# One load of x moves from SyncE's queue to GpSimd's, behind two accumulating transfers

## The chip, the cores and the metric

The kernel runs on one core of one Trainium2 chip. A core has five engines that run side by side: TensorE (PE in the profile; its weight loads are PEld), VectorE (DVE), ScalarE (ACT), GpSimd (POOL) and SyncE (SP). Sixteen DMA engines move data between the chip's large memory and the core's on-chip memory. A transfer is issued by one of the engines; those of SP and of GpSimd go through different queues, and both are served by the same sixteen DMA engines. The metric is the device time of one execution in microseconds (us), as a median over runs. Lower is better.

## What is computed

The input x has 8 batches of 4224 rows of 192 numbers. A causal convolution over the rows with 7 taps comes first: the 192 columns are 8 heads of 24, and each head has one set of softmaxed tap weights. Its result y is then normalized over the 192 columns, multiplied by a 192 x 768 matrix, cut at zero, multiplied by a 768 x 192 matrix, and added to y.

```python
w = np.exp(weight - weight.max(-1, keepdims=True)); w /= w.sum(-1, keepdims=True) + 1e-09
x_unf = x_pad[:, idx, :].reshape(B, S, K, H, group)       # 7 shifted copies of x
y = np.einsum('hk,bskhg->bshg', w, x_unf).reshape(B, S, D)
xn = (y - mu) / np.sqrt(var + 1e-06) * g_ln
out = y + np.maximum(xn @ w_ch1, 0.0) @ w_ch2
```

All of it is in 32-bit floats.

## The kernel before

**Groups.** The 4224 rows of a batch are spread over the 128 partitions, 33 consecutive rows to each. A group is a stretch of these 33 rows (n rows on every partition). Batch 0 is cut into groups 0 to 3 with n = 6, 7, 8 and 12; each later batch into two with n = 16 and 17. That makes 18 groups. Group 4 (16 rows) and group 5 (17 rows) are batch 1.

**Steps of a group.** `load_x` brings the rows of x and the six rows ahead of them into a tile `xg`, of which there are two buffers: x of group 5 takes the buffer of x of group 3. `first_tap` (L336, ScalarE) multiplies x by tap 0 into the tile `y`, also with two buffers, so that y of group 5 takes the buffer of y of group 3. `second_tap` multiplies by tap 1 into a separate tile `tb` (L349, ScalarE) and adds that to y by two accumulating transfers issued by GpSimd (L352), one for each half of the rows. `conv` adds the other taps on VectorE (L363), one instruction for each tap and head, `transpose` (L374, VectorE) turns y for the matmuls, and `store_y` (L431) writes y to the output. `up` makes the 768 hidden values on TensorE (L473), and ScalarE cuts them at zero into the tile `ht` (L485), in six blocks. The down step multiplies back (L509 or L553), and the scaled result is added to the output by accumulating transfers of GpSimd (`add_to_out`, L630).

**Two down steps.** Groups 0 to 2 use a plain one (`down`). From group 3 on `down_fast` does with seven smaller products (L553, 72 matmuls each) what would take eight. For these it needs sums and differences of quarters of `ht`, which VectorE makes (`half_sum`, L531, three instructions each). One is made ahead of the products; three are made behind the fourth product, in place, over quarters that the earlier products have read. The fifth product reads the first of these. Between the products ScalarE copies each result out (L558), and a few of the first and second taps of the group two ahead stand between these copies in its program (`some_taps`).

**Order.** It is written out by hand, and each engine works through its own program in that order. In the main loop, iteration g loads x of group g + 2, does `up(g)` on TensorE, meanwhile the taps of group g + 1 on VectorE, and then the down step of group g. Iteration 2 is the last with the plain down step: there both taps of group 4 are made whole on ScalarE (`first_tap(4)`, `second_tap(4)`), and y of group 3 is stored by GpSimd's queue, behind the two accumulating transfers. In iteration 3 VectorE does taps 2 to 4 of group 4 (24 instructions), the first half sum, taps 5 and 6 (16 instructions), the transpose, and then the three half sums of group 3's down step. The first tap of group 5 comes in that down step, on ScalarE behind the copies of the first product.

**Queues.** SP's program has the loads of x and nearly all stores of y. GpSimd's has the accumulating transfers of the second taps and of the output, and the one store of y of group 3. A transfer that has to wait (for a buffer, for data) holds up all that stands behind it in the program of the engine that issues it.

Of the kernel before, what the change touches and what calls it, by code (L numbers as in the profile page):

```python
# [16 lines left out]
def kernel(  # L17
# [27 lines left out]
    nc = tc.nc  # L45
# [27 lines left out]
    NG = len(groups)  # L73
# [25 lines left out]

    xg = {}  # L100

    def load_x(g):
        b, j0, n = groups[g]
        t = xpool.tile([P, J + PAD, D], F32, tag="xg", name=f"xg{g}")
        xg[g] = t
        flat = t.rearrange("p j d -> p (j d)")
        if j0:
            nc.sync.dma_start(
                out=flat[:, 0 : (n + PAD) * D], in_=xr[b, :, (j0 - PAD) * D : (j0 + n) * D]
            )  # L110
            return
        if b:

            nc.sync.dma_start(
                out=flat[:, 0 : (PAD + n) * D],
                in_=bass.AP(
                    tensor=x.tensor, offset=(b * S - PAD) * D, ap=[[R * D, P], [1, (PAD + n) * D]]
                ),
            )
            nc.gpsimd.memset(t[0:1, 0:PAD, :], 0.0)  # L120
            return
        nc.gpsimd.memset(t[0:1, 0:PAD, :], 0.0)
        nc.sync.dma_start(out=flat[:, PAD * D : (PAD + n) * D], in_=xr[b, :, 0 : n * D])
        for p0, p1 in ((16, P), (1, 16)):
            nc.sync.dma_start(  # L125
                out=flat[p0:p1, 0 : PAD * D],
                in_=xr[b, p0 - 1 : p1 - 1, (R - PAD) * D : R * D],
            )
# [196 lines left out]
    def first_tap(g, on_act=True, heads=(0, H)):  # L325
        n = groups[g][2]
        if g == 1:

            y[g] = y[0][:, groups[0][2] :]
        elif heads[0] == 0:  # L330
            y[g] = ypool.tile([P, J, D], F32, tag="y", name=f"y{g}")
        for h in range(*heads):
            cs = slice(h * GRP, h * GRP + GRP)
            dst, src, tap = y[g][:, 0:n, cs], xg[g][:, 0:n, cs], taps[:, h, 0:1]
            if on_act:
                nc.scalar.mul(dst, src, tap)  # L336
            else:
                nc.vector.tensor_scalar(out=dst, in0=src, scalar1=tap, scalar2=None, op0=ALU.mult)
# [3 lines left out]
    def second_tap(g, heads=(0, H)):  # L342

        n = groups[g][2]
        if heads[0] == 0:
            tb[g] = bpool.tile([P, J, D], F32, tag="tb", name=f"tb{g}")
        for h in range(*heads):
            cs = slice(h * GRP, h * GRP + GRP)
            nc.scalar.mul(tb[g][:, 0:n, cs], xg[g][:, 1 : 1 + n, cs], taps[:, h, 1:2])  # L349
        if heads[1] == H:  # L350
            for j1, j2 in ((0, n // 2), (n // 2, n)):
                nc.gpsimd.dma_start(  # L352
                    out=y[g][:, j1:j2].rearrange("p j d -> p (j d)"),
                    in_=tb[g][:, j1:j2].rearrange("p j d -> p (j d)"), accum_op=ALU.add,
                )

    def conv(g, k0=1, k1=K, heads=H):
        n = groups[g][2]
        t = xg[g]
        for k in range(k0, k1):  # L360
            for h in range(heads):
                cs = slice(h * GRP, h * GRP + GRP)
                nc.vector.scalar_tensor_tensor(  # L363
                    out=y[g][:, 0:n, cs], in0=t[:, k : k + n, cs], scalar=taps[:, h, k : k + 1],
                    in1=y[g][:, 0:n, cs], op0=ALU.mult, op1=ALU.add,
                )

    def transpose(g):
        n = groups[g][2]
        if g == 1:  # L370
            yt[g] = yt[g - 1][:, groups[0][2] :]
        else:
            yt[g] = tpool.tile([P, J, NC, C], F32, tag="yt", name=f"yt{g}")
        nc.vector.transpose(  # L374
            yt[g][:, 0:n].rearrange("p j c t -> p (j c t)"),
            y[g][:, 0:n].rearrange("p j d -> p (j d)"),
        )
# [3 lines left out]
    def moments(g):  # L381

        n = groups[g][2]
        if g % 2:
            sums[g] = sums[g - 1][:, groups[g - 1][2] :]
        else:
            sums[g] = spool.tile([P, 2 * J, nc.vector.BN_STATS_DIM], F32, tag="st", name=f"st{g}")
        for j in range(n):
            nc.vector.bn_stats(out=sums[g][:, j, :], in_=y[g][:, j, :])  # L389
# [39 lines left out]
    def store_y(g, queue=nc.sync):  # L429
        b, j0, n = groups[g]  # L430
        queue.dma_start(  # L431
            out=outr[b, :, j0 * D : (j0 + n) * D], in_=y[g][:, 0:n].rearrange("p j d -> p (j d)")
        )
# [61 lines left out]
    def down(g):  # L495


        n = groups[g][2]
        t = ht[g][1]
        po[g] = []  # L500
        order = [(c, js) for c in range(NC) for js in blocks(g)]
        if g + 1 == NG:
            order = [(c, slice(fast[g], n)) for c in range(NC)]
        for c, js in order:
            w = (js.stop - js.start) * C
            bank = psum.tile([P, 512], F32, tag="ps", name=f"po{g}_{c}_{js.start}")
            for f in range(NF):
                for q in range(NQ):
                    nc.tensor.matmul(  # L509
                        bank[C * q : C * q + C, 0:w], w2[:, f, C * c : C * c + C],  # L510
                        t[:, f, q, js.start - fast[g] : js.stop - fast[g], :],
                        start=(f == 0), stop=(f == NF - 1),
                    )
            po[g].append((c, js, bank[:, 0:w]))
# [3 lines left out]
    def w2_sums():  # L518
        (b11, b12), (b21, b22) = (
            (w2[:, e * FC : e * FC + FC, 0 : D // 2], w2[:, e * FC : e * FC + FC, D // 2 : D])  # L520
            for e in range(2)
        )

        for dst, a, b in ((0, b12, b11), (1, b22, 0), (2, b22, b12), (3, b21, 1)):
            a, b = (w2sums[:, v] if isinstance(v, int) else v for v in (a, b))
            nc.vector.tensor_tensor(w2sums[:, dst], a, b, op=ALU.subtract)
# [78 lines left out]
    def park(g):  # L605

        n = groups[g][2]
        room = 3 * CH * NFAST * T if g == 0 else NC * NFAST * C
        parked = cpool.tile([P, room], F32, tag="cs" if g else "part", name=f"parked{g}")
        parked = parked[:, 0 : NC * n * C].rearrange("p (c t) -> p c t", c=NC)  # L610
        for i, (c, js, src) in enumerate(po[g]):
            nc.scalar.copy(parked[:, c, :], src)
            po[g][i] = (c, js, parked[:, c, :])
# [37 lines left out]
    def finish(g):  # L651
        ot = ots[g] if fast[g] else out_tile(g)
        left = {}
        for c, js, src in po.pop(g):
            nc.vector.transpose(  # L655
                ot[:, js, C * c : C * c + C], src.rearrange("p (j t) -> p j t", t=C)
            )
            left[js.start] = left.get(js.start, 0) + 1
            if g + 1 == NG and left[js.start] == NC - 1:
                add(g, js, slice(0, D - C))  # L660
            if g + 1 == NG and left[js.start] == NC:
                add_and_store(g, js, D - C)
# [12 lines left out]
    join_words(w2flat, *words_2)  # L675
    store_y(0)
    for g in range(NG):
        if g + 2 < NG:
            load_x(g + 2)
        up(g)  # L680
        last = g + 1 == NG
        if not fast[g]:

            conv(g + 1)
            transpose(g + 1)
            if g < 2:
                store_y(g + 1)
                moments(g)
            first_tap(g + 2)
            if g == 2:  # L690

                second_tap(g + 2)
                store_y(g + 1, nc.gpsimd)
            down(g)
            park(g)
            if g == 1:
                finish(0)
                root(0)
                w2_sums()
                moments(2)  # L700
                finish(1)
            elif g == 2:
                moments(3)
                root(2)
                finish(2)
            continue
        if not last:
            conv(g + 1, 2, 5)
        half_sum(g, (1, 0), (0, 0), (1, 0), ALU.subtract)
        if not last:  # L710
            conv(g + 1, 5, K)
            transpose(g + 1)
            if g + 2 < NG:
                store_y(g + 1)
        parts = down_fast(g)
        if not last:

            moments(g + 1)
            if g % 2 == 0:
                root(g)  # L720
        for half in range(last, 2):
            finish_fast(g, half, *parts)
        if last:
            add_and_store(g, slice(0, fast[g]))
            down(g)
            finish(g)
# [30 lines left out]
```

## Time and profile before

| what | us |
|---|---|
| median of 4 runs | 1013.58 (1012.26 to 1014.95) |
| the four runs | 1012.34, 1014.81, 1012.26, 1014.95 |
| the profiled execution, whole | 1012.34 |
| its span, from first to last instruction | 1010.6 |
| TensorE busy in the span | 995.7 |
| VectorE busy | 844.7 |
| ScalarE busy | 561.2 |
| GpSimd busy | 62.6 |

The times of instructions come from the one profiled execution and count from the start of its span. TensorE's granted clock is 1.00 throughout. The chain of work that ended last is followed back from the last instruction, at each step to whatever released it. An idle time in square brackets behind an instruction is that of its engine just before it, with what ended it. For transfers the profile tells when they were issued and how long after that they landed; this includes any time that they stood in a queue.

### The profile page before, as it was taken

To read this page: it belongs to the slowest core of one execution; us is meant where nothing else is said; L and a number is where in the kernel's file an instruction comes from. 1 tells how busy PE (TensorE), PEld (TensorE's weight loads), DVE (VectorE), ACT (ScalarE), POOL (GpSimd) and SP (SyncE) were. 2 spreads that over 40 slices of the span, in tenths; PEclk is the share of its full clock that TensorE was granted. 3 is DMA by queue.
4 is the path that set the end of the run, shared out by engine and by line. 5 is a ranking of instruction groups with operands and counts; after the bars stand their busy time and mean duration, and the time that the engine had idled before them with its cause. 6 is when DMAs were issued, how large, how long until landed. Compare 5 with 4: busy or idle time off the path is not lost.

```text
span 1010.6 us, 35711 instructions
## 1 busy us (share of the span) xinstructions
PE 995.7 (99%) x16060; PEld 662.1 (66%) x16060; DVE 844.7 (84%) x1556; ACT 561.2 (56%) x1472; POOL 62.6 (6%) x88
## 2 busy tenths in 40 slices
PE   7999999999999999999999999999999999999997
PEld 5888665578545775458754686556854578545786
DVE  6999798899688988889689896899978899788607
ACT  5646564556546464665646556465654646554451
POOL 1001000000000000001000000000001000000000
PEclk9999999999999999999999999999999999999999
DMA  6253744633446353353633545355253734142031
GB/s 192 81 194 67 210 131 118 172 97 54 161 85 206 66 136 118 59 194 68 209 68 56 189 77 181 68 132 156 37 178 70 220 67 96 52 80 38 2 65 69
DMA packets 16102, 114.17 MB, mean 113 GB/s; under 512 B 2127, under 2 KB 2895, under 8 KB 11854
## 3 DMA queue, kind: packets, MB, share of 16 engines
q0 software_dynamic: 9072, 48.17, 25.8%
q1 hardware_dynamic: 6574, 63.73, 16.1%
q8 instruction: 125, 2.05, 0.8%
q14 instruction: 27, 0.22, 0.1%
q10 hardware_dynamic: 304, 0.00, 0.0%
HBM read 38.95 MB, written 50.23 MB: 88 GB/s over the span
## 4 chain that ended last, share of the span: by engine, by line
PE 97%; DMA 1%; DVE 1%; ACT 0%; issue 0%; SPq 0%; DVEq 0%
PE ph L473 51%; PE pd L553 40%; PE po L509 5%; DMA xg<-in_x_dram 1%; DMA ga<-in_moe_g_ln_dram 1%; ACT w L307 0%; PE pc L273 0%; DVE ht L531 0%; DVE y L638 0%; DVE yt L374 0%; PE pm L285 0%; PE pw L297 0%; PE pw L302 0%; DVE ot L655 0%; SPq L125 0%
## 5 line engine op out<-in xcount | busy, mean ns | idle before, releaser
L473 PE MATMUL ph<-yt,w 32*128 32x256 f32 (+6 forms) x7200 | 517.1, 443 | 0.4 <-DVE yt L374 0.4
L473 PEld LDWEIGHTS ph<-yt,w 32*128 32x128 f32 x7200 | 363.2, 185 | 150.9 <-issue 116.5
L363 DVE SCALAR_TENSOR_TENSOR y<-xg,taps,y 128x384 f32<-128x384 f32 (+5 forms) x740 | 367.1, 575 | 35.2 <-issue 35.1
L485 ACT ACTIVATE ht<-ph 128x256 f32<-128x256 f32 (+6 forms) x600 | 222.6, 458 | 228.8 <-PE ph L473 228.0
L531 DVE TENSOR_TENSOR ht<-ht 128x1024 f32<-128x1024 f32 (+2 forms) x180 | 205.5, 1210 | 107.1 <-PE pd L553 76.3
L553 PE MATMUL pd<-ht,w2sums 128*32 128x256 f32 (+2 forms) x4320 | 237.1, 377 | 2.0 <-DVE ht L531 2.0
L553 PEld LDWEIGHTS pd<-ht,w2sums 128*32 128x32 f32 x4320 | 140.1, 110 | 93.8 <-DVE ht L531 3.2
L553 PE MATMUL pd<-ht,w 128*32 128x256 f32 (+2 forms) x3240 | 182.0, 378 | 0.0
L553 PEld LDWEIGHTS pd<-ht,w 128*32 128x32 f32 x3240 | 103.8, 110 | 73.9 <-issue 8.3
L558 ACT COPY cs<-pd 128x256 f32<-128x256 f32 (+2 forms) x180 | 66.4, 369 | 101.8 <-PE pd L553 101.8
L626 ACT ACTIVATE ot<-ot,r 128x192 f32<-128x192 f32 x247 | 93.1, 471 | 0.0
L558 ACT COPY part<-pd 128x256 f32<-128x256 f32 (+2 forms) x135 | 49.3, 367 | 73.7 <-PE pd L553 73.7
L336 ACT ACTIVATE y<-xg,taps 128x384 f32<-128x384 f32 (+5 forms) x142 | 73.3, 591 | 4.6 <-DVE st L389 4.3
L389 DVE BATCH_NORM_STATS2 st<-y 128x6 f32<-128x192 f32 x264 | 70.2, 344 | 0.0
L349 ACT ACTIVATE tb<-xg,taps 128x384 f32<-128x384 f32 (+1 forms) x112 | 63.4, 619 | 0.0
L630 POOL DMA_DIRECT2D out_dram<-ot x34 | 29.7, 888 | 481.2 <-ACT ot L626 271.1
L601 DVE STREAM_TRANSPOSE ot<-cs 128x512 f32<-128x512 f32 (+2 forms) x90 | 56.7, 679 | 2.2
L374 DVE STREAM_TRANSPOSE yt<-y 128x3072 f32<-128x3072 f32 (+5 forms) x18 | 56.0, 3112 | 2.4 <-ACT w L307 0.5
L509 PE MATMUL po<-ht,w 128*32 128x192 f32 (+3 forms) x1152 | 51.4, 339 | 0.0
L352 POOL DMA_DIRECT2D y<-tb x28 | 24.9, 1048 | 353.8 <-ACT cs L558 175.6
L509 PEld LDWEIGHTS po<-ht,w 128*32 128x32 f32 x1152 | 37.1, 110 | 13.7 <-issue 0.8
L599 DVE TENSOR_TENSOR cs<-cs,part 128x768 f32<-128x768 f32 (+2 forms) x30 | 27.7, 925 | 0.0
(73 smaller groups left out, 150.4 us busy)
## 6 DMA issues: line engine op xcount, KB each, us to landing
y<-tb POOLq DMA_DIRECT2D x21, 768.0 KB, 6.7
xg<-in_x_dram SPq DMA_DIRECT2D x7, 2208.0 KB, 13.1
out_dram<-ot POOLq DMA_DIRECT2D x20, 768.0 KB, 6.6
xg<-in_x_dram SPq DMA_DIRECT2D x7, 2112.0 KB, 13.0
out_dram<-y SPq DMA_DIRECT2D x7, 1536.0 KB, 8.6
out_dram<-y SPq DMA_DIRECT2D x6, 1632.0 KB, 7.5
y<-tb POOLq DMA_DIRECT2D x7, 864.0 KB, 10.0
out_dram<-ot POOLq DMA_DIRECT2D x6, 864.0 KB, 7.0
```

Source lines behind the costliest of these rows:

```text
L336: nc.scalar.mul(dst, src, tap)
L349: nc.scalar.mul(tb[g][:, 0:n, cs], xg[g][:, 1 : 1 + n, cs], taps[:, h, 1:2])
L363: nc.vector.scalar_tensor_tensor(out=y[g][:, 0:n, cs], in0=t[:, k : k + n, cs], scalar=taps[:, h, k : k + 1], in1=y[g][:, 0:n, cs], op0=AL ...
L389: nc.vector.bn_stats(out=sums[g][:, j, :], in_=y[g][:, j, :])
L473: nc.tensor.matmul(ph[q][:, 0:w], w1[rows, c, fs], t[rows, js, c, :], start=(c == 0), stop=(c == NC - 1),)
L485: nc.scalar.activation(dst, src, AF.Relu)
L509: nc.tensor.matmul(bank[C * q : C * q + C, 0:w], w2[:, f, C * c : C * c + C], t[:, f, q, js.start - fast[g] : js.stop - fast[g], :], start ...
L531: nc.vector.tensor_tensor(a[:, *dst, f], a[:, *left, f], a[:, *right, f], op=op)
L553: nc.tensor.matmul(dst[C * q : C * q + C, 0:w], right[:, f, C * c : C * c + C], left[:, f, q], start=(first and f == 0), stop=(f == FC - 1 ...
L558: nc.scalar.copy(to[:, c], dst[:, 0:w].rearrange("p (j t) -> p j t", t=T))
L601: nc.vector.transpose(ot[:, 0:n, C * c : C * c + C], cs[:, c].rearrange("p j h t -> p j (h t)"))
L626: nc.scalar.mul(ots[g][:, j, :], ots[g][:, j, :], rstd[g][:, j : j + 1])
```

## The change

The load of x of group 5 is no longer issued by SP at the start of iteration 3. GpSimd issues it in iteration 2, behind the two accumulating transfers of group 4's second tap and ahead of the store of y of group 3. All other loads of x stay with SP, and nothing is added to or taken from the computation. Group 5 does not start a batch (`j0` is 16), so that its load is the single transfer of the branch shown, without a memset.

```diff
-    def load_x(g):
+    def load_x(g, queue=nc.sync):
         b, j0, n = groups[g]
         t = xpool.tile([P, J + PAD, D], F32, tag="xg", name=f"xg{g}")
         xg[g] = t
         flat = t.rearrange("p j d -> p (j d)")
         if j0:
-            nc.sync.dma_start(
+            queue.dma_start(
                 out=flat[:, 0 : (n + PAD) * D], in_=xr[b, :, (j0 - PAD) * D : (j0 + n) * D]
             )
             return
...
     for g in range(NG):
-        if g + 2 < NG:
+        if g + 2 < NG and g != 3:
             load_x(g + 2)
         up(g)
...
             if g == 2:
 
                 second_tap(g + 2)
+                load_x(g + 3, nc.gpsimd)
                 store_y(g + 1, nc.gpsimd)
```

## The prediction

> **What bounds the kernel now.** I read the page's chain of work first. It is TensorE (PE) almost from end to end, so time can only come from the few places where the chain leaves PE.
>
> ```profile
> PE 995.7 (99%) x16060; PEld 662.1 (66%) x16060; DVE 844.7 (84%) x1556; ACT 561.2 (56%) x1472; POOL 62.6 (6%) x88
> ...
> PE 97%; DMA 1%; DVE 1%; ACT 0%; issue 0%; SPq 0%; DVEq 0%
> ```
>
> Then the same chain in order of time (start, us, what). Between the first 29 us and the last 7 us it leaves PE once, in group 3: the seven products of its down step run as four, then a hole filled by three VectorE half sums, then three. From group 4 on (not shown) the seven are one piece of 504 matmuls.
>
> ```profile
> 135.69 11.88 PE pd L553 x288
> 147.57 0.02 issue
> 147.60 0.33 ACT part L558
> 147.92 0.00 issue
> 147.93 2.66 DVE ht L531 x3
> 150.59 0.04 issue
> 150.63 8.33 PE pd L553 x200
> 158.97 31.11 PE ph L473 x288
> ```
>
> Why the half sums are late is read from VectorE's timeline (start, us, then in brackets the idle time before). From 120.66 on it has no gap: 24 taps of group 4, three half sums, 16 taps, the transpose, and then the half sums PE waits for. So the hole at 147.6 is decided at 120.66, after 6.51 us of idleness.
>
> ```profile
> 112.06 2.08 DVE L655 STREAM_TRANSPOSE ot<-parked 128x256 f32<-128x256 f32 x6
> 120.66 12.79 DVE L363 SCALAR_TENSOR_TENSOR y<-xg,taps,y 128x384 f32<-128x384 f32 x24 [6.51 <-issue]
> 133.36 2.69 DVE L531 TENSOR_TENSOR ht<-ht 128x768 f32<-128x768 f32 x3
> 135.97 8.55 DVE L363 SCALAR_TENSOR_TENSOR y<-xg,taps,y 128x384 f32<-128x384 f32 x16
> 144.62 3.38 DVE L374 STREAM_TRANSPOSE yt<-y 128x3072 f32<-128x3072 f32 x1
> 147.93 7.87 DVE L531 TENSOR_TENSOR ht<-ht 128x768 f32<-128x768 f32 x9
> ```
>
> What ended that idle time is in the answers on tile tb, first for 100 to 120 us, then for the same two transfers of group 6 at 213 to 232 us (they are of the same size).
>
> ```profile
> who waited for it (us, times):
>   DVE y L363: 6.5, 1
> ...
> DMA to landing us min/median/max: 10.8/12.3/13.7
> ```
> ```profile
> DMA to landing us min/median/max: 5.7/7.6/9.5
> ```
>
> The accumulating transfers of group 4's second tap are issued from 106.2 and 106.7 us and take 10.8 and 13.7 us; the later lands at 120.4, and VectorE starts 0.26 us after. In group 6 they take 5.7 and 9.5. What differs is in the timelines of SP and GpSimd and in the DMA answer for 100 to 125 us (KB each, us from issue to landing): x of group 5 is on its way through the same DMA engines.
>
> ```profile
> 103.11 0.33 SPq L108 DMA_DIRECT2D xg<-in_x_dram  x1
> ```
> ```profile
> 106.17 1.77 POOL L352 DMA_DIRECT2D y<-tb  x2 [8.24 <-ACT parked L612]
> 107.27 1.22 POOL L431 DMA_DIRECT2D out_dram<-y  x1
> ```
> ```profile
> xg<-in_x_dram SPq DMA_DIRECT2D x1, 2208.0 KB, 10.9
> y<-tb POOLq DMA_DIRECT2D x2, 768.0 KB, 12.3
> out_dram<-y POOLq DMA_DIRECT2D x1, 1152.0 KB, 16.0
> ```
>
> **The change, part by part.** *Removed: SP's issue at 103.11.* SP does nothing else until 144.55, so its 0.33 us are worth nothing. What counts is that 2208 KB no longer occupy the DMA engines from 103.1 to 114.0 (10.9 us after the issue), ahead of and beside the accumulates.
>
> *The accumulates.* With the engines free of x, I give them group 6's latencies: the second is issued at 106.7 and lands at 106.7 + 9.5 = 116.2. Bounds: slowest by group 7's pair, whose second transfer has 864 KB and takes 10.9 us, 117.6; fastest by group 5's pair, where 864 KB take 9.3 us, 116.0; and, if x's load is not the cause at all, 120.4 as now. I take 116.2, since size and queue are the same. VectorE starts at 116.2 + 0.26 = 116.5 instead of 120.66: 4.2 us earlier.
>
> *VectorE's row behind it.* 12.79 us of taps end at 129.3. The first three half sums need the relu of hidden blocks 0 to 2, which ScalarE ends at 124.10 + 1.64 = 125.7, so they don't wait. Then 2.69 + 8.55 + 3.38 and small gaps: the transpose ends at 147.9 - 4.2 = 143.7. The next half sums overwrite what the third product reads. By the timeline of PE three products of 72 matmuls end at 144.4, and in group 4 VectorE begins its half sums about 0.5 us before the third product's end. So they start at about 144.0, and here PE, not VectorE, ends the wait. They need 0.89 us each: ready at 144.9, 145.8, 146.7, and PE asks for the first at 147.55.
>
> *PE.* Its hole closes. Seven products at 11.88 / 4 = 2.97 us are 20.8 us; from 135.69 they end at 156.5, where before they ended at 158.97: **2.5 us** less. PE's idle time in the waits gives 1.37 + 0.33 + 0.34 = 2.04, the lower figure, as it counts the sixteen matmuls that ran between the waits. I take 2.45. Closing the hole wholly needs only that the half sums start by 147.93 - 2.4 = 145.5, so a VectorE start up to 118.2 gives the same; even the slow bound 117.6 + 0.26 does. A faster accumulate brings no more than that. After 159 us the chain is unbroken PE to 1003.8, so the 2.45 us reach the end whole; no other wait takes its place.
>
> *Added: GpSimd's issue of x, and two queues it moves past.* Its row shows 0.9 to 1.2 us an issue. GpSimd is idle from 108.5 to 126.71, so the store of y of group 3 goes out some 1.2 us later at no cost on that engine. The load needs its buffer free of group 3's taps, which ended at 103.1: no new wait for GpSimd. Who waits for x of group 5? ScalarE's first tap, at 139.04, between the copies of the down products. That tap also needs the buffer of y of group 3, so it waits for that store as well. In the queue stand now: accumulates (to 116.2), x (2208 KB), store (1152 KB). The trace has no load by GpSimd. Fast bound: y's store, which landed 123.3 - 120.4 = 2.9 us after the transfer ahead of it, 397 KB per us: x in 5.6 us, store in 2.9, done at 124.7. Slow bound: the second accumulate of group 6, which lands 225.3 - 221.0 = 4.3 us after the first, 179 KB per us: x in 12.3, store in 6.4, done at 134.9. I take 10.9 us for x, which SP's load took, and 2.9: 130.0, so 9 us of cover, and 4 by the slow bound. Cost: 0.
>
> [...] The nearest row for a GpSimd transfer of plain data is the 16.0 us of y's store, against 5.9 for SP's only 1152 KB store. [...] The row of 13.7 against 9.5 us speaks of order, not of bandwidth, and I go by that row. [...]
>
> *Small parts.* The add of group 2's output is issued at 126.7 and 134.4 as before and queues at most behind y's store; its source tile is next written at 160.6. SP's store of group 4 and load of group 6 (144.55 and 145.06) come about 4 us earlier, since VectorE does; they land before the next accumulates at 157.8. 0.
>
> **Sum.** The profiled execution took 1012.34 us around a span of 1010.6 (1.74 outside). 1012.34 - 2.45 = 1009.9. It is the lower of two pairs of runs (1012.3 and 1014.9); the median is 1013.58, 1.24 above. Against the median: 1013.58 - 2.45 = **1011.1**, which I predict: -0.24%. A measurement tells about 0.3% (3.0 us) from no change, so this forecast lies just inside.
>
> **The rivals.** *A, nothing moves.* The accumulates are late for a reason other than x: for instance they wait for ring or memory work that the new order keeps, or x's packets, now right behind them, slow their tail. For it: the 13.7 us also hold y's store behind them, which stays, and which in group 6 is not there. Against: in the slices of 2 us from 106 to 120 the DMA engines are busy without a break (shares of 0.8 to 1.2), and x's 2208 KB are the largest item. VectorE starts at 120 to 121: 1013.6, plus or minus 0.5.
>
> *B, slower.* The load or y's store comes too late for ScalarE's first tap at 139.04; the tap blocks the copies behind it in ScalarE's row, and PE waits for these before it writes the bank again. It decides from a landing of y's store at about 139 + 2.0 of PE's cover + 2.45 of the gain = 143.5, that is, x and the store taking 27 us behind the accumulates, where the slow bound has 18.7. At twice the slow bound (37.4 us) the store lands at 153.6, the loss is 153.6 - 141 = 12.6 us and the time 1013.6 - 2.45 + 12.6 = 1023.7.
>
> *C, more than forecast.* The 2.6 us by which two of the runs are longer may be this same hole, larger in them (nothing in the one profile shows it). Then all runs of the changed kernel are at 1009.9, 3.7 us or 0.36% under the median. Against: the start, too, hangs on DMA landings, and would vary alike.
>
> **How the numbers follow.** Forecast 0.55, C 0.22, A 0.11, B 0.12. The forecast's median may fall between its own pairs, 1009.9 to 1012.4, so of its 0.55 about 0.15 is beyond 0.3%. Faster: 0.15 + 0.22 = 0.37; within: 0.40 + 0.11 = 0.51; slower: 0.12. Range: from 1009.1 (C and 0.8 of scatter) to 1014.3 (A with its scatter); it leaves out B and little else.
>
> **What would show it.** In the changed profile: the two accumulates landing 6 and 9.5 us after issue; VectorE's first 24 taps of group 4 starting near 116.5 with an idle time of 2 to 3 us; the half sums released by PE; the seven products of group 3 as one piece of 504; the step up of group 4 starting near 156.5; ScalarE's first tap of group 5 still at 139.0. I am wrong if those 24 taps still start at 120, or if ScalarE idles before 139 for a DMA.

## The result, and the profile after

The changed kernel takes 1011.21 us (median of 42 runs, 1010.45 to 1012.93), the kernel before 1012.95 (median of 64 runs, 1011.59 to 1015.46). The ratio is 0.9981 (95% interval 0.9977 to 0.9986): 1.9 us or 0.19% less (the two medians differ by 1.74 us), inside the 0.3% bound and below no change by every value of the interval. The prediction was 1011.1 us and 0.24% less.

Two things are seen in the times that the medians hide. The slowest run of the changed kernel, 1012.93, lies below the median of the kernel before. And 29 of the 64 runs of the kernel before lie above 1013.5, none of the 42.

The chain of work of the changed kernel around group 3 (start, us, what):

```profile
136.62 9.93 PE pd L553 x240
146.55 0.05 issue
146.59 2.67 DVE ht L531 x3
149.26 0.04 issue
149.31 2.53 PE pd L553 x56
151.83 0.02 issue
151.85 0.33 ACT cs L558
152.18 0.05 issue
152.23 6.06 PE pd L553 x144
158.29 31.11 PE ph L473 x288
```

The hole of 3.06 us is gone, but two small ones are left, and the products are not one piece of 504. (The chain goes back over VectorE's half sums from 146.59 on; TensorE itself works on till 149.1, as its timeline below shows.) All of group 3 stands 0.92 us later than in the first profile of before, because the start of the program took that much longer in this execution (more on that below). So I compare lengths, from TensorE's first matmul of group 3's up step to its first of group 4's. They are read from TensorE's timeline, first of the kernel before, then of the changed one:

```profile
112.19 23.50 PE L473 MATMUL ph<-yt,w 32*128 32x384 f32 x288
150.63 5.41 PE L553 MATMUL pd<-ht,w2sums 128*32 128x192 f32 x128 [0.34 <-DVE ht L531]
158.90 6.29 PE L473 MATMUL ph<-yt,w 32*128 32x512 f32 x56
```
```profile
113.11 23.50 PE L473 MATMUL ph<-yt,w 32*128 32x384 f32 x288
149.31 2.48 PE L553 MATMUL pd<-ht,w2sums 128*32 128x192 f32 x56 [0.20 <-DVE ht L531]
152.23 3.13 PE L553 MATMUL pd<-ht,w2sums 128*32 128x192 f32 x72 [0.45 <-ACT cs L558]
158.22 7.15 PE L473 MATMUL ph<-yt,w 32*128 32x512 f32 x64
```

That is 46.71 and 45.11 us, **1.60 less**. Without any wait the stretch would be 23.43 + 7 x 2.97 = 44.22 us.

VectorE's timeline of the changed kernel, and the answer on tile tb for 100 to 120 us:

```profile
113.09 2.08 DVE L655 STREAM_TRANSPOSE ot<-parked 128x256 f32<-128x256 f32 x6
119.32 12.79 DVE L363 SCALAR_TENSOR_TENSOR y<-xg,taps,y 128x384 f32<-128x384 f32 x24 [4.16 <-issue]
132.03 2.69 DVE L531 TENSOR_TENSOR ht<-ht 128x768 f32<-128x768 f32 x3
134.63 8.55 DVE L363 SCALAR_TENSOR_TENSOR y<-xg,taps,y 128x384 f32<-128x384 f32 x16
143.29 3.38 DVE L374 STREAM_TRANSPOSE yt<-y 128x3072 f32<-128x3072 f32 x1
146.59 7.87 DVE L531 TENSOR_TENSOR ht<-ht 128x768 f32<-128x768 f32 x9
```
```profile
DMA to landing us min/median/max: 5.9/8.7/11.5
```

The first accumulate lands after 5.9 us, as in group 6 (5.7). The second takes 11.5, between the 13.7 of before and group 6's 9.5. VectorE idles 4.16 us where it idled 6.51. Everything behind it has the same durations as before, without a gap.

GpSimd's timeline and the DMA answer for 100 to 140 us (KB each, us from issue to landing) show the price of the new order:

```profile
107.09 1.78 POOL L352 DMA_DIRECT2D y<-tb  x2 [8.22 <-ACT parked L612]
108.19 1.24 POOL L108 DMA_DIRECT2D xg<-in_x_dram  x1
108.74 1.22 POOL L431 DMA_DIRECT2D out_dram<-y  x1
```
```profile
xg<-in_x_dram POOLq DMA_DIRECT2D x1, 2208.0 KB, 17.8
y<-tb POOLq DMA_DIRECT2D x2, 768.0 KB, 8.7
out_dram<-y POOLq DMA_DIRECT2D x1, 1152.0 KB, 20.0
```

x lands at 108.2 + 17.8 = 126.0 and y's store at 108.7 + 20.0 = 128.7, both far ahead of ScalarE's first tap of group 5, which stands at 139.96, right behind its copy. They cost nothing.

### The profile page after: what moved, and what is told of

It reads as the page before. It is cut to its first block, busy times and chain, and to the rows that moved or that the text cites. A ratio compares the mean times of both kernels' runs of the same rounds, so it can differ in the third digit from the quotient of the medians.

```text
span 1010.0 us, 35712 instructions
## 1 busy us (share of the span) xinstructions
PE 996.0 (99%) x16060; PEld 662.5 (66%) x16060; DVE 844.7 (84%) x1556; ACT 561.0 (56%) x1472; POOL 63.5 (6%) x89
## 3 DMA queue, kind: packets, MB, share of 16 engines
q8 instruction: 125, 2.05, 0.8%
## 4 chain that ended last, share of the span: by engine, by line
PE 98%; DVE 1%; DMA 1%; ACT 0%; issue 0%; SPq 0%; DVEq 0%
PE ph L473 51%; PE pd L553 40%; PE po L509 5%; DMA room<-in_moe_w_ch_dram 1%; PE pc L273 0%; PE idle L313 0%; DVE ht L531 0%; PE pw L297 0%; PE pm L282 0%; DVE y L638 0%; PE pw L302 0%; PE pm L285 0%; DVE room L205 0%; DVE room L197 0%; ACT room L189 0%; DVE ot L655 0%
## 5 line engine op out<-in xcount | busy, mean ns | idle before, releaser
L509 PEld LDWEIGHTS po<-ht,w 128*32 128x32 f32 x1152 | 37.1, 110 | 13.7 <-issue 0.8
```

What stands on the lines that cost most here:

```text
L509: nc.tensor.matmul(bank[C * q : C * q + C, 0:w], w2[:, f, C * c : C * c + C], t[:, f, q, js.start - fast[g] : js.stop - fast[g], :], start ...
```

## The experiments

**Is it the order or the queue?** My theory was order: x must not stand ahead of or beside the accumulates. The rival was that x only has to leave SP's queue. One kernel keeps x on SP, but behind the accumulates; one moves x to GpSimd, but ahead of them. In the first, `probe` stores a corner of y of group 4 that both accumulates write; SP has to wait for them there and so issues x only after they have landed. The differences shown are against the changed kernel, if nothing else is said.

```diff
+    def probe(src):
+        nc.sync.dma_start(out=outr[groups[4][0], 0:16, 0:D].rearrange("p (a d) -> p a d", a=2), in_=src)
...
                 second_tap(g + 2)
-                load_x(g + 3, nc.gpsimd)
                 store_y(g + 1, nc.gpsimd)
+                mid = groups[g + 2][2] // 2
+                probe(y[g + 2][0:16, mid - 1 : mid + 1, D // 2 : D])
+                load_x(g + 3)
```

> x of group 5 is issued by SP again, but only when both accumulates of group 4 have landed (a small store of a corner of y of group 4, overwritten later, stands ahead of it in SP's program and waits for them); y of group 3 is stored by GpSimd behind the accumulates, as in the kernel before. If order is what counts (x must not stand ahead of or beside the accumulates), the second accumulate lands 9.5 to 10.5 us after its issue, VectorE's taps of group 4 idle 2.5 to 3.5 us, the hole in group 3's products closes, x lands at about 128, and the time is 2.0 to 2.5 us below the kernel before. If the queue is what counts (x must leave SP's queue), the accumulates have the latencies of before (10.8 and 13.7) and the time does not change.

Measured: 1010.88 us, ratio 0.9979 (0.9970 to 0.9988), 2.1 us less. Accumulates 5.8 and 11.2 us, group 3's stretch 44.96 us. x was issued at 118.39 and landed 9.0 us later.

```diff
-    def second_tap(g, heads=(0, H)):
+    def second_tap(g, heads=(0, H), ahead=None):
...
+        if ahead:
+            ahead()
         if heads[1] == H:
             for j1, j2 in ((0, n // 2), (n // 2, n)):
...
-                second_tap(g + 2)
-                load_x(g + 3, nc.gpsimd)
+                second_tap(g + 2, ahead=lambda: load_x(g + 3, nc.gpsimd))
                 store_y(g + 1, nc.gpsimd)
```

> x of group 5 is issued by GpSimd, but ahead of the two accumulates, not behind them. If order counts, the second accumulate lands 13 to 15.5 us after its issue, the hole is as in the kernel before or up to 1.5 us larger: 0 to +1.5 us. If leaving SP's queue counts, it is as the changed kernel: 1.9 us below the kernel before.

Measured: 1014.25 us, ratio 1.0013 (1.0004 to 1.0023), 1.3 us more. In its profile TensorE's clock is at half from 149.95 to 153.37 us, from the end of the hole on (TensorE resumes at 150.05); what that costs comes further down. The answer on tile tb of this kernel:

```profile
DMA to landing us min/median/max: 11.8/13.3/14.9
```

The queue is not the cause: with x on GpSimd but ahead, the accumulates are even later than before (14.9 against 13.7), and with x on SP but behind them, they are as early as in the changed kernel. Order is what counts.

**What keeps the second accumulate at 11.5 us?** The next two take away what stands right behind it: first x, by having y's store go between, then both.

```diff
                 second_tap(g + 2)
-                load_x(g + 3, nc.gpsimd)
                 store_y(g + 1, nc.gpsimd)
+                load_x(g + 3, nc.gpsimd)
```

> As the changed kernel, with GpSimd's order accumulates, store of y of group 3, x of group 5. If the 2 us by which the second accumulate still is late in the changed kernel (11.5 us against 9.5 in group 6) come from x standing right behind it, it now lands after 9.5 to 10.5 us and the time is 2.2 to 2.5 us below the kernel before. If any large transfer behind it costs the same, it stays near 11.5 and the time near 1.9 below. x lands before 128, so nothing waits for it.

Measured: 1011.13 us, ratio 0.9981 (0.9972 to 0.9991); second accumulate 11.1 us, stretch 45.51. The time is that of the changed kernel, the landing lies between my two cases.

The other has, behind `second_tap`, the `probe` and then `load_x(g + 3)` and `store_y(g + 1)`, all on SP.

> Both x of group 5 and the store of y of group 3 are issued by SP when the accumulates of group 4 have landed, so that these have the DMA engines to themselves. The second accumulate lands 9.5 us after its issue, as in group 6; the seven products are one piece; 2.45 us below the kernel before (the whole hole). x lands near 128 and the store near 131, ahead of ScalarE's first tap at 139. If the residue of the changed kernel is not from transfers behind, the second accumulate stays at 11.5 and the time near 1.9 below.

Measured: 1011.14 us, ratio 0.9983 (0.9975 to 0.9992). I had expected the whole 2.45 us; it is 1.7. Its answer on tile tb, and its chain of waits around the products:

```profile
DMA to landing us min/median/max: 5.7/8.4/11.1
```
```profile
135.83 14.84 PE pd L557 x360
150.67 0.02 issue
150.69 0.33 ACT cs L562
151.02 0.66 issue
151.68 6.06 PE pd L557 x144
```

Both halves of the expectation failed. With nothing behind it in any queue the second accumulate still takes 11.1 us. And though VectorE's half sums now come in time, so that five products run without a gap, TensorE pauses 1.01 us before the sixth.

For the landing, the packet records of the trace show where the time is. In them each of the two accumulates ends with sixteen packets of 4 bytes, called reports here (in the changed kernel from 112.43 to 112.61 us and from 116.93 to 118.06), and the landing comes behind the last of them. The table has the reports of the second accumulate, the fifteenth and the last, and the end of the one 16 KB packet of the profile's "instruction" queue of that moment, all in us after the first accumulate's last report. (The last two rows are of kernels that follow below.)

```
kernel                        15th    last    end of the instruction packet
before, group 6               3.69    4.23    5.21, it starts at the last report
nothing behind                3.70    5.10    5.11
x behind, on SP               3.71    5.12    5.13
x behind the store            3.72    5.11    5.12
changed kernel                4.76    5.46    5.47
changed kernel, again         4.76    5.53    5.01
nothing behind, shifted       3.70    5.23    3.29
x late                        3.70    5.13    5.15
```

Without x right behind, the first fifteen reports come as early as in group 6, to 0.03 us: so far it is the 9.5 us of the prediction. The sixteenth comes 1.4 us behind them, and in five rows within 0.02 us of the end of the instruction packet. Which of the sixteen DMA engines carried what the records don't tell, and this is a coincidence in time and not an experiment: the changed kernel's second profile doesn't fit it, and in the shifted kernel the last report is 1.5 us late though the packet was over before the fifteenth. Nor is the late report all: in nothing behind the landing follows it by 1.2 us, in group 6 by 0.5. Why the second accumulate doesn't reach 9.5 us stays open; the shifted kernel, with nothing behind either, has 10.4. What x right behind does is seen: the fifteen come 1.06 us later with it (4.76 against 3.70), most of which the sixteenth hides.

**The pause before the sixth product.** Next I shifted TensorE's program by 16 matmuls and left all else of nothing_behind as it was.

```diff
-    keep_warm(20)
+    keep_warm(36)
```

> The kernel with nothing behind the accumulates, and 16 more of the warming matmuls whose result nobody reads, early in the program, so that every later matmul stands 16 places further on in TensorE's program. There TensorE paused 1.0 us between the fifth and the sixth product of group 3, waiting for nothing that the profile shows, and resumed 0.8 us after a 16 KB packet of the instruction queue had ended. If it is the supply of instructions that comes late, the pause moves by about 16 matmuls (0.6 to 1.3 us) to an earlier place, now inside the fifth product, or goes; if it is a wait of the sixth product for a copy or a half sum, it stays exactly between the fifth and the sixth.

The chain of the shifted kernel:

```profile
136.12 13.46 PE pd L557 x328
149.59 1.30 issue
150.89 7.36 PE pd L557 x176
158.25 31.11 PE ph L477 x288
```

The pause is now behind 328 instructions and not 360, inside the fifth product, where the profile shows no wait for anything (1.30 us of "issue"). 32 is 16 matmuls, each of which the profile shows as two instructions. So the pause is tied to a place in TensorE's program and not to a copy or a half sum. That TensorE had no instructions there is my reading; no trace shows it. The pause of nothing behind is at the same place as the one that the chain of the changed kernel puts down to ScalarE's copy (0.40 us in the first profile, 0.77 in the second). That copy isn't waited for: in the kernel before it runs from 153.19 to 153.51, while TensorE's 128 matmuls from 150.63 on (shown above) go through it without a gap.

```profile
153.19 0.32 ACT L558 COPY cs<-pd 128x192 f32<-128x192 f32 x1 [0.66 <-PE pd L553]
```

The profile has a queue that it names "instruction" (q8: 125 packets and 2.05 MB in the execution of before, 16 KB each), and every pause, of 0.18 to 1.31 us, comes behind a late packet of it. What else moves between these kernels and those without a pause is when SP stores y of group 4 and loads x of group 6. The times are us after the first matmul of group 3's products:

```
kernel                     SP issues    16 KB packet       TensorE's
                           the store    of instructions    pause
before                     8.93          9.35 to 10.39     none
before, hole half filled   8.78          9.24 to 10.57     none
changed kernel             6.67         13.31 to 14.24     15.24 to 15.69
changed kernel, again      6.29         13.49 to 14.42     14.86 to 15.68
x behind, on SP            6.79         13.23 to 14.16     15.36 to 15.54
x behind the store         6.31         13.72 to 14.65     14.88 to 16.09
nothing behind             6.30         13.70 to 14.66     14.87 to 15.92
nothing behind, shifted    5.58         12.42 to 13.35     13.53 to 14.84
```

With VectorE earlier, the store and the load behind it (1536 and 2112 KB) go out 2 to 3 us earlier. In the kernel before the packet starts ahead of their data, on idle DMA engines (share 0.00 from 140 to 144 us, the packet from 144.97); in the changed kernel's second profile the share is 0.97 from 146 to 149 us and 1.05 from 149 to 152, and the packet comes 4 us later (from 149.11), in the midst of them. TensorE resumes 1.3 to 1.5 us behind the packet's end in all six (1.26 in nothing behind, not the 0.8 of the expectation). The row of the half-filled hole (the last experiment below) shows that it isn't TensorE's standing still that gave the packet its time: there TensorE doesn't stand still, the packet starts at 9.24, and there is no pause. No run moves SP's two transfers alone, so that they put off the packet is read from the traces and not tried.

**What does it cost if x comes too late?** Rival B of the prediction, provoked: x is issued by SP only behind ScalarE's last scaling of group 2.

```diff
         up(g)
+        if g == 3:
+            probe(ots[2][0:16, groups[2][2] - 1, :])
+            load_x(5)
...
-                load_x(g + 3, nc.gpsimd)
```

(`probe` here stores one row of 16 partitions.)

> x of group 5 is issued by SP only when ScalarE has made the last scaling of group 2 in group 3's up step (about 134.3 us), much later than in any other kernel, to price rival B of the prediction. x alone took 9.0 us from SP, so it lands at about 143.5 to 145.5, 4 to 6 us after ScalarE's first tap of group 5 is due (139.0 to 139.9). By the prediction's formula the loss is the landing less 141 to 142: 2 to 4 us in group 3's products, while the accumulates are clean and save 1.9: -0.3 to +2.3 us against the kernel before. If ScalarE's row has more slack than I read, it is 1.9 below like the changed kernel.

Measured: 1017.13 us, ratio 1.0048 (1.0031 to 1.0065), 4.9 us more, twice the upper end of what I expected. The chain:

```profile
134.58 10.04 DMA xg<-in_x_dram
144.62 0.02 issue
144.64 0.02 ACTq L336
144.66 0.05 issue
144.70 1.68 ACT y L336 x3
146.39 0.21 ACT cs L562
146.60 0.04 issue
146.64 16.51 PE pd L557 x360
```

The mechanism is that of the prediction, but the formula was too low twice. I had let TensorE lose the landing less 141; it resumes 2.0 us behind the landing, as three taps and a copy come first, and its idle time is 4.96 us. And the five products behind it, which need 14.85 us, take 16.51, since TensorE's clock is granted at half from 146.71 to 150.12 us. That last point was new.

**Where do the long runs of before come from?** I profiled the kernel before three more times and the changed one once more.

> The kernel before, unchanged, for a second profile: its runs lie near 1012.0 and near 1014.6. If the hole in group 3 is what differs between them (rival C), a profile of a long run shows a hole larger than 3.1 us by what the run is above 1012.3, with the accumulates landing later than 13.7; if it is something else, the hole is 3.1 as in the first profile and the surplus shows at another place of the chain.

> The same once more, since one profile need not be of a long run: hole of 3.1 us and the second accumulate at 13.7 in a run near 1012.3; larger in one near 1014.6 by rival C, the same otherwise.

> The kernel before once more: hole of about 3 us; if the run is near 1012, TensorE's clock stays at full through group 3, if it is near 1014 or more, the clock is at half for 3.4 us right behind the hole (1.7 us lost), as in the profile of the run of 1013.94.

> The changed kernel, unchanged, for a second profile: the second accumulate at 11 to 11.5 us, a rest of 0.2 to 1.2 us of idle TensorE in group 3, TensorE's clock at full in group 3 whatever the run's time. A long run, if it is one, differs before 30 us.

```
profile          whole run   group 3's stretch   2nd accumulate   clock at half in group 3
before           1012.34     46.71               13.7             no
before again     1012.65     47.01               14.1             no
before again 2   1013.94     48.30               13.7             yes
before again 3   1014.90     48.28               14.1             yes
changed          1011.76     45.11               11.5             no
changed again    1010.80     45.09               11.1             no
```

TensorE's rows in stretches (busy us and instructions, granted clock, DMA share, GB/s), first of the run of 1012.34, then of that of 1013.94:

```profile
146.00:149.00 3.00, 1.63 (x44) 1.00 1.01 385
149.00:152.00 3.00, 2.33 (x52) 1.00 0.93 361
152.00:155.00 3.00, 3.00 (x80) 1.00 0.88 372
```
```profile
146.00:149.00 3.00, 1.72 (x45) 1.00 1.00 385
149.00:152.00 3.00, 2.33 (x40) 0.81 0.99 377
152.00:155.00 3.00, 3.00 (x52) 0.63 0.85 360
```

The hole is as long in both to 0.1 us, and the accumulate as late. But in the longer run TensorE's clock is granted at half right behind the hole, for 3.4 us by the trace's clock events, and 52 matmuls get through where 80 did. That costs 1.7 us: in the chain the 200 matmuls behind the hole take 10.01 us and not 8.33. In busy time it is invisible (3.00 of 3.00 us both times). So rival C was right that the long runs come from this hole, and wrong on how: not a longer hole, but the clock behind it.

In the run of 1014.90 the clock drops at 14.59 and at 151.12 us, for 3.41 us each. In the run of 1013.94 TensorE does not stand still throughout ahead of the drop: in the 3.42 us before it (147.42 to 150.84) it is busy for 43% of the time, with sixteen matmuls in the hole (0.53 us for each eight by the timeline). Nor does the longest idle piece of the hole tell the four profiles apart: it is 1.28 us in the run of 1013.94 and 1.71 in that of 1014.90, which have the drop, and 1.37 and 1.68 in the two that don't. Why two profiles have it and two don't stays open.

The record has the mean granted clock of every run, and it sorts them. Of the 72 runs of the kernel before that were taken with these experiments, 37 have 0.999 or 1.000 and take 1011.37 to 1012.97 us; 14 have 0.998 and take 1012.99 to 1014.00; 19 have 0.996 and take 1014.52 to 1015.29. The profiled run of 1013.94, with one drop, has 0.998, and that of 1014.90, with two, 0.996. Of 43 runs of the changed kernel none has 0.996. Between the runs at 0.999 or more (37 and 26), the means differ by 1.1 us, 1012.05 and 1010.98.

The changed kernel has a half clock too, in the profile of 1011.76 but not in that of 1010.80: at the start of the program, from 14.99 to 18.40 us. The profile of 1014.90 of the kernel before has it as well. In these two, group 3 begins at 113.1 and 113.2 us, in the four others at 112.2; so this is the 0.92 us of the first comparison, and the change has no part in it.

**The hole without the clock.** Last I took the kernel before, kept VectorE as late as it was and filled the hole with matmuls that nobody reads.

```diff
         product(1, a[:, 0, 1], b[2], part[:, 0], True)
         some_taps(3)
+        if g == 3:
+            fill = psum.tile([P, 512], F32, tag="ps", name="fill")
+            for _ in range(20):
+                nc.tensor.matmul(
+                    fill[:, 0:P], w2flat[:, 0:P], w2flat[:, P : 2 * P], start=True, stop=True
+                )
```

> The kernel before, with 20 matmuls of constants into an unread bank added to TensorE's program in group 3, between the fourth and the fifth product, so that they run in the hole (2.4 us of its 3.1). Group 3's wait for VectorE stays as long as it was. If the long runs of the kernel before (near 1014.5, against 1012.1) come from TensorE's clock, granted at half for 3.4 us after the idle hole, the clock no longer drops there: all runs near 1012.1, none above about 1013.5, median 0.5 to 1.2 us below that of the kernel before. If the long runs have another cause, the two humps stay and the median is the same or up to 0.5 us higher.

Measured: 1014.66 us, ratio 1.0017 (1.0009 to 1.0026). I had taken a matmul for one pass of 0.12 us; it is two such instructions, so the 20 took 4.66 us, 1.6 more than the hole. The median says nothing about the clock therefore. The spread agrees with it: 12 runs from 1014.38 to 1015.60, in two humps 0.8 us apart, as the start alone makes them (the profile of 1015.20 has the clock at 0.94 in the first 29 us and at 1.00 in every later stretch up to 1000). The same with 10 matmuls:

> As the kernel before with its hole filled, but with 10 matmuls of constants, not 20: each was two passes of 0.117 us, so that 20 took 4.66 us and stood 1.6 us over the hole; 10 take 2.33 us and fit. VectorE is as late as in the kernel before. If the clock's drop behind the hole is what makes the long runs, no run has it: two close humps that only the start makes, near 1012.1 and 1012.9, the highest below 1013.5, median 0.5 to 1.0 us below that of the kernel before. If not, runs at 1014 and more remain, with the median of the kernel before. Of the changed kernel's gain this would be the clock's share; the rest, some 1 to 1.2 us, is the hole itself.

Measured: 1012.41 us (1012.21 to 1014.01, 11 runs), ratio 0.9998 (0.9989 to 1.0007). The profile has the fill in the hole, TensorE without a pause in group 3 and the clock at full, stretch 46.61. Ten of the eleven runs lie between 1012.21 and 1013.24, and none above 1014.2, where 4 of the 15 runs of the kernel before on the same chip lie. One, at 1014.01 with a mean clock of 0.998, I can't explain; it was not profiled. The expected gain in the median is missing: in this series the median of the kernel before was itself a run at full clock (1012.27, mean clock 1.000). By the means it is 1012.70 against 1012.93. So the fill takes away most of the long runs and, with the clock on record for each run, supports the clock as their cause, but of its share in the median it proves nothing.

## Why the prediction was right, and where a term was off

The sign and the place were right, and most steps stand in the profile as written, in the order in which they were written. That the time was met to 0.1 us (1011.1 foretold, 1011.21 measured) is luck: the gain was put at 2.45 us where the ratio gives 1.9, and the median of the kernel before, taken from four runs, at 1013.58 where 64 runs give 1012.95; the two errors cancel.

- *Removed: SP's issue; x no longer ahead of the accumulates.* Right, and shown by the two kernels that part order from queue.
- *The accumulates.* Mis-sized. Group 6's 9.5 us were foretold; 11.5 and 11.1 were measured, within the bounds (9.3 for group 5's pair, 13.7 as before), but above the slowest row of the kind that I had, 10.9. The limit that I gave for closing the hole (a start of VectorE at 118.2, that is a landing after 11.2) held: at 11.1 it is closed, at 11.5 a little is left. With nothing behind it is still 11.1 (10.4 in the shifted kernel), so it isn't x alone that keeps it from group 6's 9.5; the late sixteenth report is part of it, its cause is open.
- *VectorE's row behind it.* Right to 0.1 us in every duration. It starts 2.3 us earlier than before relative to the end of its transposes, not 4.2. So the half sums were not released by PE, as foretold, but start when VectorE's own transpose ends (146.59 in the first changed profile, where all stands 0.92 later, 145.29 in the second; foretold 144.0).
- *PE.* 2.45 us foretold; 1.60 and 1.62 between profiles without a drop of the clock. Of the missing 0.9 us, the rest of the hole and the pause before the sixth product (0.40) share it in the first changed profile; in the second the hole is closed and the pause alone is 0.77: a wait that took the place of the one removed, which the prediction didn't have. "No other wait takes its place" was the sentence that failed. The term behind it is one of the small parts: that SP's store of group 4 and load of group 6 come earlier was foretold (by 4 us; it is 2.3 and 2.6) and put at 0, with an eye on the next accumulates alone. In the traces a packet of the instruction queue comes 4 us later with them, ahead of the pauses of 0.40 and 0.77 us; that the one makes the other was not shown.
- *The clock.* Not foreseen. It adds to the gain: 1.7 us in those runs of before that have the drop. By the clocks on record, 1.1 of the 1.9 us is what runs at full clock gain, and the rest, an estimate of 0.8, comes from the runs of before with a drop. That 1.1 is less than the 1.60 of the profiles: the runs at full clock of the kernel before, at 1012.0, lie some 0.3 to 0.6 us below those that were profiled without a drop, and why is open.
- *Added: x behind the accumulates, y's store behind x.* Right: x took 6.9 us more from issue to landing than on SP (17.8 against 10.9), y's store 4.0 more (20.0 against 16.0), all of it covered. Done at 128.7 (127.8 on the clock of the first profile, where group 3 stands 0.92 earlier), where I had said 130.0 (bounds 124.7 and 134.9).
- *Against it* stood the row of y's store, 16.0 us on GpSimd where SP's took 5.9. Another issuer alone was worth nothing: with x on GpSimd ahead of the accumulates the time was 1014.25 us, ratio 1.0013. Order was worth the change.
- *Rival A* fell, the accumulates moved. *Rival B* didn't occur; provoked, it cost more than its formula says. *Rival C* had the right place and the wrong mechanism; its 0.36% did not come, since 35 of the 64 runs of before lie below 1013.5, so that its median is not one of the long runs.

## What to carry to other kernels

When one engine is late at one place only, look for the transfer it waited for and then for what else was on the DMA engines: moving a load that had over 20 us to spare behind the one that had none cost nothing here, on GpSimd's queue or on SP's. A hole on the bounding engine is not worth its own length: it may be worth more, if the clock drops behind it in some runs (here by 1.7 us in two profiles of four; a spread with two humps is a hint, and the granted clock shows it where busy time doesn't), and less, if a smaller wait was hidden under it (here 1.60 us were gained of 3.06). Before calling a hole closed, ask what the bounding engine would wait for next (here it paused for 0.18 to 1.31 us, for no copy and no half sum), and what the engine that is now earlier sends out earlier.

## What the runs showed of the hardware that I had not expected

- Behind a hole of 3.0 us on TensorE, with sixteen matmuls in it, the granted clock was at half for 3.4 us in two profiles of four, at 1.7 us each, and busy time did not show it (3.00 of 3.00 us, 52 matmuls where 80 were done).
- TensorE paused in a straight piece of program, for 0.2 to 1.3 us, at a place that moved with the program and not with the data (360 instructions before it, 328 when the program was 32 longer), 1.3 to 1.5 us behind a 16 KB packet of the profile's "instruction" queue that came 3 to 4 us later than in the kernel before, amid 3.6 MB of other transfers.
- The last of the sixteen reports of the second accumulate came 0.5 to 1.5 us behind the fifteenth, and in five of the seven profiles with x behind the accumulates this coincided with the end of a packet of the instruction queue.
